# Sliding-window attention and a mixture of adapters on one core: rows of q and k laid on the partitions run by run instead of head by head

## The chip, the cores and the metric

The kernel runs on one core of a Trainium2 chip. The metric is the device time of one execution in microseconds (us); the times of several runs are summed up by their median. The core has TensorE (PE, matrix products; PEld is its weight load), VectorE (DVE), ScalarE (ACT), GpSimd (POOL) and SyncE (SP). SP, ACT and POOL issue the transfers (DMAs), which 16 DMA engines of the core carry out.

## The reference

`q`, `k` and `v` have the shape 8 batches x 8 heads x 576 positions x 64, in float32. The first part is attention in a window of 32 positions to each side, the second a mixture of eight low-rank adapters of which each row takes the best two:

```python
scores = scale * np.matmul(q, k.transpose(0, 1, 3, 2))
mask = np.abs(pos[:, None] - pos[None, :]) <= window          # window = 32
attn = softmax(np.where(mask, scores, -1e9))
x = (attn @ v).transpose(0, 2, 1, 3).reshape(4608, 512)
logits = x @ w_gate                                            # 8 experts
# the two largest logits of a row, softmax over the two: w
out = x + sum over the two experts e of  w_e * (x @ A[e]) @ B[e]    # A: 512x16, B: 16x512
```

## The kernel before, in words

**Tiling.** The batches are taken in two groups (`g` = 0, 1; four batches each), and a step handles one batch `s` of each group, for all eight heads: four steps, `s` = 0 to 3. The 576 positions of a batch are cut into tiles: for each `s` a tile t = 2s (256 positions) and t = 2s + 1 (the next 256), and one more tile, t = XT = 8, that holds the 64 left-over positions of all batches and heads together.

**Loads of q and k** (`run_parts`, `load_qk`; DMA issue in line 308). The rows of a tile are cut in runs of eight positions, 8 x 64 x 4 B = 2 KB in one piece. Even and odd runs go to two buffers (`f` = 0, 1), and for each of them and each group there is one DMA: 128 runs on 128 partitions, 256 KB. For t < 8 the 128 runs are 8 heads by 16 runs, and line 286 puts the head outermost: partition = 16 h + n. For t = XT there are 32 (batch, head) pairs by 4 runs (k, 256 KB) or by 2 runs (q, which takes 32 positions from each end, 64 partitions, 128 KB). In all there are 64 DMAs of 256 KB for t < 8, and 4 of 256 KB and 8 of 128 KB for XT. All are issued by SP, one after the other, in a queue that also holds the 40 stores of the output (line 648).

**From the load to the scores.** A cast to float16 (`cast`: line 321 on POOL or DVE, line 319 on ACT) puts both groups beside each other in `c16`; TensorE transposes it in eight products of 128 x 128 against the identity matrix `ident` (line 329), so that the 64 features stand on the partitions and the partition number of the load becomes the column; ACT or DVE copies the result from PSUM to `qT` or `kT` (line 345). Then, for each step and each of nine key blocks, TensorE writes the mask (line 416) and the scores of all heads (line 422) to PSUM, ACT takes the exponential (line 428), TensorE multiplies with v (line 468), DVE normalises (lines 480, 487).

**Loads of v** (`load_v`, line 373): four DMAs of 128 KB (as written) for each tile, issued by POOL, converted to float16 on the way, then turned by DVE (line 381).

**Adapters** (`moe`): TensorE turns the normalised rows (513), multiplies them with gate and A (553), DVE and ACT work out the gates (563 to 594), TensorE turns again (603), multiplies with B (627) and, from s = 1 on, adds x by a product with the identity (630); ACT or DVE copies to `ob` (638, 641), SP stores.

**What sets the order.** Every operation is entered in a plan with an index. Three tables written out by hand or by a search, `ORDER`, `ON` and `HOME`, say in which order the operations are issued, which of two engines takes one that either can do, and which buffer each tile lives in (9 buffers `raw`, 6 `c16`, 3 `v16`, 8 PSUM banks). Each engine works through its own instructions strictly in that order.

Of the kernel before, what the change touches and what calls it, by code (L numbers as in the profile page):

```python
# [9 lines left out]
F16 = mybir.dt.float16  # L10
F32 = mybir.dt.float32
AF = mybir.ActivationFunctionType
ALU = mybir.AluOpType
# [5 lines left out]
NH = 8  # L19
# [35 lines left out]
class Plan:  # L55
# [14 lines left out]
    def op(self, eng, dur, fn, bufs=(), need=(), make=(), prio=0.0, dma=0.0, mode=0, count=0, desc=0):  # L70
        eng = eng if isinstance(eng, dict) else {eng: dur}
        o = Op(eng, fn, list(bufs), list(need), list(make), prio, dma)
        o.mode, o.count, o.desc = mode, count, desc
        self.ops.append(o)
        for b in o.bufs:
            b.ops.append(o)
        for m in o.make:
            self.makers.setdefault(m, []).append(o)
        return o
# [24 lines left out]
def kernel(  # L104
# [50 lines left out]

    ident = sb.tile([128, 128], F16, name="ident")
    twice = sb.tile([128, 128], F16, name="twice")
    mask0 = sb.tile([128, 128], F16, name="mask0")
    mask = sb.tile([128, 128], F16, name="mask")
    wgf = sb.tile([128, 4, E], F32, name="wgf")  # L160
# [12 lines left out]
    def mm(n): return n / 2400.0 + 0.0035  # L173
# [8 lines left out]


    op("POOL", 0.6, lambda: make_identity(nc, ident), make=["ident"], prio=-99)

    def build_mask():
        nc.gpsimd.memset(mask0, 0.0)
# [91 lines left out]
    def run_parts(w, t, f):  # L279

        r = []
        for g in range(2):
            x = grows[w][g]
            if t < XT:
                r0 = 256 * (t % 2) + (32 if w == "q" else 0)
                i = x[t // 2, :, r0:r0 + 256].rearrange("h (n f r) d -> f h n (r d)", f=2, r=8)[f]
                r.append((g, 0, 128, i))
            elif w == "k":
                i = x.rearrange("b h n d -> (b h) n d")[:, 512:576].rearrange(
                    "u (n f r) d -> f u n (r d)", f=2, r=8)[f]  # L290
                r.append((g, 0, 128, i))
            else:
                for e in range(2):
                    i = x.rearrange("b h n d -> (b h) n d")[:, 544 * e:544 * e + 32].rearrange(
                        "u (n f r) d -> f u n (r d)", f=2, r=8)[f]
                    r.append((g, 64 * e, 64, i))
        return r

    def load_qk(w, t):
# [5 lines left out]
        for hf in range(2):  # L305
# [21 lines left out]
            def trans(c16=c16, tp=tp):  # L327
                for r in range(8):
                    nc.tensor.matmul(out=ap16(tp)[:, 128 * r:128 * r + 128], lhsT=ap(c16)[:, r],  # L329
                                     rhs=ident, is_transpose=True, start=True, stop=True)  # L330
            pr = due - 22 + late + 0.1 * hf
            op("PE", 8 * mm(128), trans, bufs=[c16, tp], need=[(w, t, hf, "16"), "ident"],
               make=[(w, t, hf, "T")], prio=pr, count=8)

            def evict(eng, hf=hf, tp=tp):
# [333 lines left out]
def BY_PE(s, w, j):  # L669
# [2 lines left out]


ORDER = (
# [31 lines left out]
)  # L706
ON = (
    "000011100000010000110010000000000000000001000000000000010100100000001000001000001000010000"
    "001000110010000000000000000000000000000100010100100000010000000100000000000010001010000100"
    "000000000000000000000000000000000000000000000000000100000000000000010000000000000000010000"  # L710
    "000000000000010010010000000010000000000000010000000000000000101100000000101000010000000000"
    "000000010000000000000000000000000000000000100000011010000000000000100000100100000000000000"
    "000000100100000000000000000000000001000001000000000000000000000000000000010000000000000000"
    "000000000000000000000000000000000000010000010000000000"
)
HOME = (
# [13 lines left out]
)  # L730


# [28 lines left out]
```

## Time and profile before

| | |
|---|---|
| median of three runs | 178.53 us (176.23 to 179.34) |
| profiled execution, its own time | 178.09 us |
| its span | 176.3 us, so 1.8 us lie around the span |
| PE busy | 123.9 us (70%) |
| DVE, ACT, POOL busy | 89.9, 86.3, 50.9 us |
| mean granted clock of PE | 0.868 |
| bytes from and to memory | 28.85 MB read, 9.44 MB written |

The span is counted from the first instruction. "DMA" in a list of slices or windows is the mean busy share of the 16 DMA engines (1.00: all of them, all the time), GB/s what they moved. In a row of the timeline the two numbers ahead are the start and the length in us; a row of several instructions says how many ("x3"). The chain is the work that ended last, followed back to what released it.

### The profile page before, as it was taken

How to read it: one execution, taken by the hardware profiler on the slowest of the kernel's cores; microseconds unless marked ns; L12 is line 12 of the kernel's file. 1: busy time of each engine (PE TensorE's matmuls, PEld its weight loads, DVE VectorE, ACT ScalarE, POOL GpSimd, SP SyncE). 2: the span in 40 equal slices, each digit the busy share in tenths (PEclk: the TensorE clock that was granted, in tenths of full speed). 3: DMA queues.
4: the chain of work that ended last, by engine and by line, in shares of the span. 5: the costliest groups of instructions: out<-in, count | busy, mean ns of one | idle time of the engine just before them, and what ended most of it. 6: DMA issues, size and time to landing. Idle time of an engine off the chain costs nothing.

```text
span 176.3 us, 5204 instructions
## 1 busy us (share of the span) xinstructions
PE 123.9 (70%) x2206; PEld 89.6 (51%) x2206; DVE 89.9 (51%) x186; ACT 86.3 (49%) x123; POOL 50.9 (29%) x85
## 2 busy tenths in 40 slices
PE   4800487629619879469998997807947999986660
PEld 2200465526419757456588765504736776675220
DVE  3002182703612797184998675521235959767720
ACT  4000356334802768155866876307345779742540
POOL 8700006284237368002403580029602000000000
PEclk9995559975985999957999999965699999999997
DMA  3876656779659569865556669778939030373086
GB/s 108 192 185 221 180 184 221 216 211 232 152 187 241 159 204 227 190 242 211 204 208 256 229 191 244 264 277 272 231 101 321 0 122 14 124 231 106 26 308 204
DMA packets 19272, 33.91 MB, mean 192 GB/s; under 512 B 4145, under 2 KB 4145, under 8 KB 19249
## 3 DMA queue, kind: packets, MB, share of 16 engines
q1 hardware_dynamic: 15168, 28.32, 45.7%
q0 software_dynamic: 2752, 4.72, 15.8%
q10 hardware_dynamic: 1328, 0.54, 1.1%
q8 instruction: 17, 0.28, 0.6%
q14 instruction: 7, 0.05, 0.1%
HBM read 28.85 MB, written 9.44 MB: 217 GB/s over the span
## 4 chain that ended last, share of the span: by engine, by line
DMA 58%; PE 24%; DVE 7%; SPq 3%; ACT 3%; issue 1%; POOLq 1%; DVEq 0%; ACTq 0%
DMA raw<-in_q_dram 35%; DMA raw<-in_k_dram 23%; PE banks L422 5%; PE banks L468 4%; SPq L308 3%; PE banks L513 3%; PE banks L627 3%; PE banks L329 3%; PE banks L416 3%; DVE xb L487 2%; PE banks L630 2%; PE banks L553 1%; DVE ob L641 1%; PE banks L603 1%; DVE zs L594 1%
## 5 line engine op out<-in xcount | busy, mean ns | idle before, releaser
L321 POOL CAST c<-raw 128x1024 f16<-128x1024 f32 x26 | 27.1, 1053 | 82.1 <-DMA raw<-in_q_dram 37.3
L329 PE MATMUL banks<-ident,c 128*128 128x128 f16 x288 | 26.2, 251 | 26.5 <-ACT c L319 15.1
L428 ACT ACTIVATE PT<-banks 128x1024 f16<-128x1024 f32 x36 | 35.7, 1025 | 10.0 <-PE banks L422 9.6
L329 PEld LDWEIGHTS <-c 128*128 128x128 f16 x288 | 21.0, 113 | 30.2 <-ACT c L319 16.6
L422 PE MATMUL banks<-qT,kT 64*64 64x128 f16 (+1 forms) x576 | 24.5, 230 | 1.2 <-ACT qT L355 1.0
L422 PEld LDWEIGHTS <-kT 64*64 64x64 f16 x576 | 18.7, 116 | 10.9 <-issue 9.9
L381 DVE STREAM_TRANSPOSE vt<-v 128x1024 f32<-128x1024 f32 x9 | 18.6, 2063 | 10.9 <-DMA v<-in_v_dram 10.9
L638 ACT COPY ob<-banks 128x1024 f32<-128x1024 f32 x13 | 13.0, 1013 | 18.5 <-issue 7.4
L416 PE MATMUL banks<-mask,twice 64*128 64x512 f16 x72 | 15.6, 427 | 8.5 <-ACT ob L638 7.3
L319 ACT CAST c<-raw 128x1024 f16<-128x1024 f32 x7 | 7.3, 1045 | 27.3 <-DMA raw<-in_k_dram 14.3
L468 PE MATMUL banks<-vt,PT 64*128 64x65 f16 x832 | 17.8, 194 | 3.8 <-ACT ob L638 2.4
L373 POOL DMA_DIRECT2D v<-in_v_dram x36 | 19.6, 559 | 0.0
L468 PEld LDWEIGHTS <-PT 64*128 64x128 f16 x832 | 15.0, 96 | 7.7 <-issue 6.0
L487 DVE TENSOR_TENSOR xb<-banks,rc 128x768 f16<-128x768 f32 x16 | 15.1, 956 | 2.0 <-PE banks L513 1.5
L627 PE MATMUL banks<-Bw,zT 128*128 128x512 f16 x40 | 15.0, 396 | 1.4 <-DVE zT L179 0.7
L480 DVE RECIPROCAL rc<-banks 128x12 f32<-128x12 f32 (+1 forms) x28 | 6.2, 220 | 15.5 <-PE banks L468 15.3
L487 DVE TENSOR_TENSOR xa<-banks,rc 128x640 f16<-128x640 f32 (+1 forms) x12 | 10.4, 869 | 5.8 <-PE banks L513 5.3
L345 ACT COPY qT<-banks 128x512 f32<-128x512 f32 x13 | 7.6, 590 | 11.8 <-PE banks L329 11.8
L181 ACT COPY xT<-banks 128x512 f32<-128x512 f32 x16 | 9.2, 588 | 6.7 <-PE banks L513 6.6
L553 PE MATMUL banks<-WA,xT 128*128 128x136 f16 x160 | 11.7, 232 | 0.2 <-ACT xT L181 0.2
L321 DVE CAST c<-raw 128x1024 f16<-128x1024 f32 x3 | 2.1, 694 | 18.6 <-DMA raw<-in_q_dram 18.6
L553 PEld LDWEIGHTS <-xT 128*128 128x128 f16 x160 | 10.5, 103 | 1.4 <-issue 0.6
(58 smaller groups left out, 126.2 us busy)
## 6 DMA issues: line engine op xcount, KB each, us to landing
raw<-in_k_dram SPq DMA_DIRECT2D x36, 256.0 KB
raw<-in_q_dram SPq DMA_DIRECT2D x32, 256.0 KB
out_dram<-ob SPq DMA_DIRECT2D x24, 256.0 KB
v<-in_v_dram POOLq DMA_DIRECT2D x36, 128.0 KB, 6.7
out_dram<-ob SPq DMA_DIRECT2D x16, 192.0 KB
raw<-in_q_dram SPq DMA_DIRECT2D x8, 128.0 KB
ob<-in_moe_B_dram ACTq DMA_DIRECT2D x1, 256.0 KB
ob<-in_moe_A_dram ACTq DMA_DIRECT2D x1, 256.0 KB
```

Source lines behind the costliest of these rows:

```text
L321: (nc.vector if eng == "DVE" else nc.gpsimd).tensor_copy(out=o, in_=i)
L329: nc.tensor.matmul(out=ap16(tp)[:, 128 * r:128 * r + 128], lhsT=ap(c16)[:, r], rhs=ident, is_transpose=True, start=True, stop=True)
L373: op("POOL", 0.5, lambda p0=p0, src=src: nc.gpsimd.dma_start(out=ap(v16)[p0:p0 + 32], in_=src), bufs=[v16], make=[("v", t, "16")], prio=-6 ...
L381: nc.vector.transpose(out=o, in_=i)
L416: nc.tensor.matmul(out=p[:, 4 * j:4 * j + 4], lhsT=twice[m], rhs=bcast(mask[m], 1, 4), start=True, stop=False)
L422: nc.tensor.matmul(out=p[m, h, c0:c0 + hi - lo], lhsT=ap(kT[t])[m, 64 * sl:64 * sl + 64], rhs=ap(qT[s])[m, h, lo:hi], start=False, stop=h ...
L428: op("ACT", act(1024), lambda: nc.scalar.activation(out=ap(pt)[:, :, 64:192].rearrange("m i (x b r) -> m i x b r", b=2, r=16), in_=ap(ps). ...
L468: nc.tensor.matmul(out=ap(po)[:, 512 * g + VD * j:512 * g + VD * j + VD], lhsT=ap(PT[ti])[m, pos, off:off + 128], rhs=ap(vt[t])[m, sl, 0:V ...
L487: nc.vector.tensor_tensor(out=o, in0=i, in1=ap(rc)[:, 0:n].to_broadcast([128, n, 2, D]), op=ALU.mult)
L553: nc.tensor.matmul(out=ap(pz)[:, o:o + ER + E], lhsT=ap(xT)[:, i, c, :], rhs=WA[:, c, :], start=(c == 0), stop=(c == 3))
L627: nc.tensor.matmul(out=o, lhsT=ap(zT)[:, j + i], rhs=Bw, start=True, stop=not by_pe)
L638: (nc.vector.tensor_copy if eng == "DVE" else nc.scalar.copy)(out=ap(ob)[:, 0:m], in_=i0)
```

## The change: 16 runs by 8 heads

For t < 8, the source of a load is now read as (run, head) instead of (head, run): run n of head h goes to partition 8 n + h. The DMAs keep their number, their 256 KB and their 2 KB pieces. So that the columns after the transpose are in the old order, the transposes of these tiles take a permutation matrix `swap` instead of `ident`; it is built once on POOL by a memset and one selection. XT keeps its layout and `ident`.

The three tables are new as a whole. On POOL, the constants are now built ahead of all loads of v, in the order mask, `ident`, `swap`, `twice`. On SP, the eight loads of t = 0 and the eight of q for XT are now the first 16 loads; before, one load of k for XT stood ahead of the last of them. Casts stay 26 on POOL, 7 on ACT and 3 on DVE; the copies to `ob` go from 13 on ACT and 2 on DVE to 11 and 4; ahead of the last load on SP stand 13 stores instead of 12. On PE, the last transpose for q or k is followed by 504 products instead of 458. Nothing else is changed; lines behind 157 move down by one and those behind 185 by some ten.

```diff
+    swap = sb.tile([128, 128], F16, name="swap")
...
+    def build_swap():
+
+        nc.gpsimd.memset(swap, 0.0)
+        blk = swap.rearrange("p (h n) -> p h n", n=16)
+        nc.gpsimd.affine_select(out=blk, in_=blk, compare_op=ALU.not_equal, fill=1.0, base=0,
+                                channel_multiplier=1, pattern=[[-1, NH], [-NH, 16]])
+    op("POOL", 0.6, build_swap, make=["swap"], prio=-98.5)
...
             if t < XT:
                 r0 = 256 * (t % 2) + (32 if w == "q" else 0)
-                i = x[t // 2, :, r0:r0 + 256].rearrange("h (n f r) d -> f h n (r d)", f=2, r=8)[f]
+                i = x[t // 2, :, r0:r0 + 256].rearrange("h (n f r) d -> f n h (r d)", f=2, r=8)[f]
...
                     nc.tensor.matmul(out=ap16(tp)[:, 128 * r:128 * r + 128], lhsT=ap(c16)[:, r],
-                                     rhs=ident, is_transpose=True, start=True, stop=True)
+                                     rhs=swap if t < XT else ident, is_transpose=True,
+                                     start=True, stop=True)
...
-            op("PE", 8 * mm(128), trans, bufs=[c16, tp], need=[(w, t, hf, "16"), "ident"],
+            op("PE", 8 * mm(128), trans, bufs=[c16, tp], need=[(w, t, hf, "16"), "ident", "swap"],
...
 ORDER = (
-    26, 23, 3, 24, 12, 10, 9, 34, 15, 40, 35, 0, 63, 6, 61, 45, 4, 39, 18, 36, 30, 29, 19, 62, 44,
...
+    25, 4, 7, 8, 18, 19, 27, 2, 26, 36, 41, 35, 15, 58, 30, 57, 40, 5, 56, 55, 45, 20, 31, 62, 65,
...
```

More of the change, by code (lines that the diff above doesn't have):

```diff
@@ L674 @@
 ORDER = (
[31 rows of a table removed]
[31 rows of a table added]
 )
 ON = (
[L708 to L714, printed above, removed]
+    "001110000000100000000100010001000000010000000010000001000100000000000000000101000100000100"
+    "001000010000000110010000000000000000100000000000000000001000100010000000000000000010000000"
+    "000000000100000000000001000000000000000000000000010001000000000000000101000000000000000000"
+    "001000001000000000000010000000000000000000000100000000000000000000010000100000100000010010"
+    "000100100000001000000000011000001000000000000010000100000000000100000100000100010010000000"
+    "000000000000000000010000000000000000000000100000000000000000000000000000000000000100000000"
+    "0000000000000000000000000000000000000000100000000001000"
 )
 HOME = (
[13 rows of a table removed]
[13 rows of a table added]
 )
```

86 rows, old and new, of tables (HOME, ORDER) are left out of this document.

## The prediction

> **What bounds the kernel now.** I read the page from the top: the busy shares, then the slices, the DMA queues, and the chain that ended last.
>
> ```profile
> span 176.3 us, 5204 instructions
> PE 123.9 (70%) x2206; PEld 89.6 (51%) x2206; DVE 89.9 (51%) x186; ACT 86.3 (49%) x123; POOL 50.9 (29%) x85
> ...
> q1 hardware_dynamic: 15168, 28.32, 45.7%
> q0 software_dynamic: 2752, 4.72, 15.8%
> q10 hardware_dynamic: 1328, 0.54, 1.1%
> ...
> DMA 58%; PE 24%; DVE 7%; SPq 3%; ACT 3%; issue 1%; POOLq 1%; DVEq 0%; ACTq 0%
> DMA raw<-in_q_dram 35%; DMA raw<-in_k_dram 23%; PE banks L422 5%; PE banks L468 4%; SPq L308 3%; PE banks L513 3%; PE banks L627 3%; PE banks L329 3%; PE banks L416 3%; DVE xb L487 2%; PE banks L630 2%; PE banks L553 1%; DVE ob L641 1%; PE
> ```
>
> No compute engine is full, and 58% of the chain is loads of q and k. Yet the DMA engines look idle a third of the time: the three queues sum to 62.6% of 16 engines. The two fit together only if the loads cannot use all engines. So I looked for a stretch in which nothing but these loads is in flight, and found 80 to 94 us. SP issues there:
>
> ```profile
> 79.06 3.23 SPq L308 DMA_DIRECT2D raw<-in_q_dram  x3
> 82.91 1.99 SPq L308 DMA_DIRECT2D raw<-in_k_dram  x2
> 85.62 0.60 SPq L308 DMA_DIRECT2D raw<-in_q_dram  x1
> 86.26 0.60 SPq L308 DMA_DIRECT2D raw<-in_k_dram  x1
> 86.95 2.86 SPq L308 DMA_DIRECT2D raw<-in_q_dram  x3
> 90.36 1.93 SPq L308 DMA_DIRECT2D raw<-in_k_dram  x2
> ```
>
> All are 256 KB loads for t < 8. POOL issues no v between 71 and 99 us. The windows show what that yields, and what stores alone yield (134 to 136 us):
>
> ```profile
> core 0: us, PE busy (x) PEld busy (x) DVE busy (x) ACT busy (x) POOL busy (x), PEclk, DMA share, GB/s
> 14.00:18.00 4.00, 0.00 (x0) 0.00 (x0) 0.17 (x2) 0.66 (x1) 0.00 (x0) 0.50 0.73 222
> 18.00:20.00 2.00, 1.56 (x15) 1.56 (x16) 0.00 (x0) 0.69 (x2) 0.00 (x0) 0.50 0.72 174
> 26.00:28.00 2.00, 2.00 (x37) 1.38 (x36) 0.87 (x1) 1.00 (x2) 1.31 (x2) 0.69 0.52 200
> 80.00:94.00 14.00, 13.46 (x315) 10.06 (x313) 11.24 (x19) 9.03 (x11) 3.08 (x3) 0.93 0.54 205
> 134.00:136.00 2.00, 1.88 (x70) 1.73 (x71) 0.56 (x2) 1.07 (x2) 0.06 (x1) 1.00 1.02 385
> ```
>
> For 14 us the share sits at 0.54 and the rate at 205 GB/s, as at 26 us (0.52, 200): half the engines, all the time. Stores reach 1.02 and 385 GB/s. The share goes well over a half only with stores, with v, or with the 128 KB loads of XT (14 to 20 us). The loads with a share of a half are those whose source has 8 heads outermost; the stores and XT have 96 or 128 rows, or 32 (batch, head) pairs, outermost. So half the DMA engines bound the kernel up to the last load, with which this stretch of the chain ends:
>
> ```profile
> 120.35 12.52 DMA raw<-in_k_dram
> ...
> 134.12 0.62 PE banks L329 x8
> ```
>
> After it come 43 us in which loads play no part. The three long stretches:
>
> ```profile
> 25.00:133.00 108.00, 81.18 (x1537) 61.42 (x1534) 57.73 (x113) 57.82 (x85) 42.92 (x59) 0.85 0.71 215
> 75.00:110.00 35.00, 31.41 (x646) 23.92 (x647) 26.57 (x58) 23.71 (x34) 10.69 (x14) 0.90 0.66 223
> 133.00:157.00 24.00, 23.03 (x545) 16.60 (x543) 18.17 (x33) 16.91 (x23) 1.04 (x1) 1.00 0.33 118
> ```
>
> From 133 to 157 us PE is full: 545 products in 24 us, 22.7 a us. While loads bind (25 to 133 us) it does 1537 in 108 us, 14.2 a us.
>
> **The change part by part.**
>
> *Loads.* With 16 runs outermost I expect each load for t < 8 to spread over all 16 engines. At 205 GB/s the 64 loads of 262,144 B take 81.8 us; at the stores' 385 GB/s, 43.6 us. So 38 us leave the path at most, and only as far as something else does not fill the room. [...]
>
> *Stage A, to the first score (25.40 us before).*
>
> ```profile
> 25.40 0.61 PE L416 MATMUL banks<-mask,twice 64*128 64x512 f16 x2
> ```
>
> ```profile
> L319 ACT CAST c<-raw 128x1024 f16<-128x1024 f32 x7 | 7.3, 1045 | 27.3 <-DMA raw<-in_k_dram 14.3 <-DMA raw<-in_q_dram 13.0
> L345 ACT COPY qT<-banks 128x512 f32<-128x512 f32 x13 | 7.6, 590 | 11.8 <-PE banks L329 11.8
> ```
>
> ```profile
> 0.00:10.00 10.00, 5.93 (x8) 2.28 (x8) 1.62 (x8) 1.99 (x3) 6.91 (x25) 1.00 0.67 158
> 22.00:25.00 3.00, 2.26 (x22) 1.89 (x21) 2.18 (x5) 1.41 (x2) 0.00 (x0) 0.50 0.60 183
> ```
>
> The start of the first score, the two groups of hand-over work (busy, mean ns) and two windows: the engines move some 4.4 MB in the first 25 us (158 GB/s at first, 174 to 222 later). XT's loads, wide already, the weights and v are among them, so I take the middle of 205 and 385, 295 GB/s: 15 us, plus 2 us until the flow stands, plus cast 1.05, transposes 0.62, copy 0.59: 19.3, called **20 us**. Ends: 16 (all at 385) and 25.4.
>
> *Stage B, to the last load (25 to 133 us before).* The DMA engines' own work there is 0.71 x 108 = 77 us at full width; PE's 1537 products at 22.7 a us need 68 us. Neither runs without gaps. From 75 to 110 us, where loads bound less, PE did 646 in 35 us, 18.5 a us; at that pace 1537 take **83 us**. It is the nearest row to a mixture of loads, casts and scores, so I take it. Ends: 77 (DMA full) and 108.
>
> *Stage C, from the last load to the end.* 176.3 - 133 = 43.3 us. The new order leaves 504 products behind the last transpose instead of 458; 46 at 22.7 a us are 2 us: **45 us**. Ends 43 and 47. It contains a serial tail (157 to 176 us) that nothing here shortens.
>
> *The transposes.* 256 of the 288 take `swap` in place of `ident`: same shape, same type, same count. Two dense stretches bound the difference:
>
> ```profile
> 96.02 0.92 PE banks L513 x16
> 96.94 0.45 PE banks L329 x8
> ```
>
> 57.5 and 56 ns each for transposes of other data: 256 x 1.5 ns is 0.4 us either way. I take 0.
>
> *POOL at the start.* `swap` adds a memset and a selection:
>
> ```profile
> masks.py:199 POOL TENSOR_SCALAR_AFFINE_SELECT ident<-ident 128x128 f16<-128x128 f16 x1 | 0.3, 289 | 0.1
> masks.py:197 POOL MEMSET ident<- 128x128 f16 x1 | 0.2, 206 | 0.3 <-POOLq L745 0.3
> ```
>
> ```profile
> 3.73 0.71 POOL L373 DMA_DIRECT2D v<-in_v_dram  x1
> 13.12 0.69 DVE L321 CAST c<-raw 128x1024 f16<-128x1024 f32 x1 [10.67 <-DMA raw<-in_q_dram]
> 24.90 1.97 DVE L381 STREAM_TRANSPOSE vt<-v 128x1024 f32<-128x1024 f32 x1
> ```
>
> 0.5 us, done by about 4 us, while the first cast starts at 13.12 us (some 9 after): hidden. The first load of v, at 3.73 us, falls behind all constants, by 2.5 us; its four pieces end behind two of another tile. The DVE turn that needs it ran at 24.90 us: hidden now. If stage A shrinks to 16, up to 2 us may show. SP keeps its 76 loads and 40 stores in one queue; 13 stores instead of 12 stand ahead of the last load, and a store that waits for its copy holds the loads behind it. One more is worth 0.5 us at the 0.3 to 0.5 us that one takes to issue, or a wait for the copy, up to 2 us; it lies inside stage B's ends. Two copies to `ob` moving from ACT to DVE (1.0 against 1.2 us each) meet engines busy half the time: 0.
>
> *Sum.* 20 + 83 + 45 = 148 us of span against 176.3; with the 1.8 us around it, **150 us** against the profiled execution's 178.09. The median, 178.53, is 0.4 us above that; I leave this out. Of the 38 us that the loads could give, 28 come through, because PE is next: in stage B its floor (68) and the DMA floor (77) are close.
>
> **The rivals.**
>
> *Wide reads run slower per engine.* In the windows from 14 to 20 us, with XT loads in the mixture, a share of 0.73 gave 222 and one of 0.72 gave 174 GB/s: weighted, 206 at 0.73, or 282 GB/s at full share, against 205 / 0.54 = 380 for the narrow loads alone. At 282 the 64 loads take 59.5 us, a gain of 22 instead of 38; in proportion 28 x 22/38 = 16 us of span: **162 us**. For it: those two rows. Against: stores at 385, and XT reads its heads outermost, which the new loads do not. The same 157 to 170 would come if PE, casts and copies hand over worse than from 75 to 110 us (16 products a us give 96 us for stage B, 163 in all).
>
> *Slower.* If the 16 engines, reading pieces 4 KB apart at the same time, hinder each other so that a wide load moves less than 205 GB/s, the change loses: that is the turning point. At the 174 of the 18 to 20 us row the 64 loads take 96.4 us, 14.6 more than now; in the same proportion +11 us: **189 us**. Nothing but that one short row, at a share of 0.72, speaks for it, and its rate per engine (174 / 0.72 = 242 at full share) is still above the turning point.
>
> *The loads do not widen.* If the spread over engines does not come from the outermost dimension, the share stays near 0.54 and only the order differs: **174 to 182 us**. Against: two kinds of load on the same queue, from the same tensors, that differ in that dimension and in the share.
>
> *Better.* If stage B reaches the DMA floor of 77 and stage A 16 us: 16 + 77 + 45 + 1.8 = **140 us**.
>
> **How the numbers follow.** Forecast, 142 to 157 us: 0.55. Wide reads slower or a worse hand-over, 157 to 172: 0.28. Below 142: 0.06. No widening, 174 to 182: 0.06. Slower: 0.05. The predicted time is 150 us. The range reaches from 140 to 170: it leaves out some 0.05 below, 0.03 of the second case, and the last two. About 2% (3.6 us) is what a measurement of this kernel can tell from no change, the three runs lying 1.7% apart. Faster by more than that: 0.89; within: 0.06; slower: 0.05.
>
> **What would show it.** Right: a window with loads for t < 8 alone has a DMA share near 1 and over 330 GB/s; the first score starts near 20 us; the last load lands near 103 us; PE does 18 products a us between them; DMA's part of the chain falls well below 58% and PE's rises. Wrong: a share near 1 with under 300 GB/s (slow wide reads), a share that stays near 0.54 (no widening), or loads that are through early with PE still at 14 to 16 products a us, which would put the bound in the order or in the casts and copies.

## The result, and the profile after

The changed kernel takes 148.27 us (median of 4 runs, 147.79 to 149.54), the kernel before beside it 178.03 (176.23 to 179.34): a ratio of 0.837 with a 95% interval of 0.827 to 0.846. The ratio is taken over executions with an undisturbed clock, so that it can differ a little from the quotient of two medians. The forecast was 150 us. The profiled execution took 149.54 us, with a span of 147.8.

The page of the changed kernel: busy shares, the two DMA rows of the 40 slices, the queues and the chain that ended last.

```profile
span 147.8 us, 5212 instructions
PE 117.6 (80%) x2206; PEld 85.0 (58%) x2206; DVE 90.4 (61%) x185; ACT 84.9 (57%) x123; POOL 51.6 (35%) x88
...
DMA  4999999999999999999999999999911030940484
GB/s 128 256 225 254 266 254 297 283 258 254 271 273 273 275 240 277 268 286 347 326 278 322 302 301 290 145 266 293 332 40 49 27 113 0 320 150 0 170 311 160
...
q1 hardware_dynamic: 15680, 28.32, 63.5%
...
PE 54%; DMA 20%; DVE 13%; ACT 3%; issue 3%; POOL 2%; SPq 0%; DVEq 0%; ACTq 0%; POOLq 0%
```

PE now has the largest part of the chain, and loads have 20% of it instead of 58% (14 points of the 20 are loads of q and k, 6 are loads of v). The DMA engines are full from 4 to 107 us (90% or more in every slice). But look at q1, the queue of all q and k loads and of all stores. It moves the same 28.32 MB as before and takes more engine time for them: 63.5% of 147.8 us is 93.9 us, against 45.7% of 176.3, which is 80.6 us. The loads have become wide (a share of 1.07 in the first two windows below, 0.54 before), and each engine has become slower: it takes longer for the same bytes.

Windows of the changed kernel (start and end, length, busy time and count of each engine, granted clock, DMA share, GB/s). In the first row only loads of q and k for t < 8 move; in the second also three loads of k for XT, which SP issues between them. Then come stages B and C of the prediction, and the same time cut at 25, 65 and 105 us:

```profile
core 0: us, PE busy (x) PEld busy (x) DVE busy (x) ACT busy (x) POOL busy (x), PEclk, DMA share, GB/s
20.00:25.00 5.00, 4.24 (x43) 3.04 (x41) 3.80 (x6) 2.22 (x3) 1.04 (x1) 0.52 1.07 293
22.00:30.00 8.00, 7.14 (x120) 4.98 (x120) 2.95 (x5) 5.64 (x7) 4.77 (x7) 0.82 1.07 292
23.80:104.50 80.70, 71.72 (x1474) 54.89 (x1474) 55.78 (x110) 54.76 (x80) 41.56 (x58) 0.95 1.04 279
104.50:147.80 43.30, 33.39 (x688) 22.78 (x680) 28.18 (x60) 23.22 (x33) 1.04 (x1) 0.96 0.39 134
...
0.00:25.00 25.00, 13.72 (x74) 8.07 (x74) 7.62 (x17) 7.49 (x11) 9.73 (x30) 0.73 0.98 239
25.00:65.00 40.00, 32.12 (x689) 25.90 (x684) 24.58 (x48) 25.78 (x39) 21.51 (x32) 0.92 1.06 265
65.00:105.00 40.00, 38.91 (x796) 28.60 (x793) 30.46 (x65) 28.39 (x41) 19.82 (x27) 0.99 1.02 293
```

The same cut of the kernel before:

```profile
25.00:65.00 40.00, 27.71 (x523) 21.21 (x520) 18.48 (x33) 19.61 (x30) 18.85 (x26) 0.80 0.71 201
65.00:105.00 40.00, 35.25 (x691) 27.21 (x690) 29.03 (x59) 25.38 (x37) 15.06 (x22) 0.91 0.68 217
```

The timeline of the changed kernel has the edges of the stages: the cast whose transposes stand ahead of the first score on PE, the first DVE turn of v, the first score, and the last cast of q, which starts when the last load has landed.

```profile
21.62 1.04 ACT L328 CAST c<-raw 128x1024 f16<-128x1024 f32 x1 [0.93 <-DMA raw<-in_q_dram]
...
23.45 1.99 DVE L391 STREAM_TRANSPOSE vt<-v 128x1024 f32<-128x1024 f32 x1
...
23.69 0.61 PE L426 MATMUL banks<-mask,twice 64*128 64x512 f16 x2
...
104.53 1.04 POOL L330 CAST c<-raw 128x1024 f16<-128x1024 f32 x1 [6.96 <-DMA raw<-in_q_dram]
```

Stage A went from 25.4 to 23.7 us, stage B (first score to last load) from 107.6 to 80.8, stage C stayed at 43.3. So 26.8 of the 28.5 us of span were gained between the first score and the last load.

### The profile page after: what moved, and what is told of

Same layout as the page of the kernel before. It is cut to its first block, busy times and chain, and to the rows that moved or that the text cites. A ratio compares the mean times of both kernels' runs of the same rounds, so it can differ in the third digit from the quotient of the medians.

```text
span 147.8 us, 5212 instructions
## 1 busy us (share of the span) xinstructions
PE 117.6 (80%) x2206; PEld 85.0 (58%) x2206; DVE 90.4 (61%) x185; ACT 84.9 (57%) x123; POOL 51.6 (35%) x88
## 3 DMA queue, kind: packets, MB, share of 16 engines
q1 hardware_dynamic: 15680, 28.32, 63.5%
## 4 chain that ended last, share of the span: by engine, by line
PE 54%; DMA 20%; DVE 13%; ACT 3%; issue 3%; POOL 2%; SPq 0%; DVEq 0%; ACTq 0%; POOLq 0%
PE banks L432 11%; DMA raw<-in_q_dram 9%; PE banks L338 8%; PE banks L478 8%; PE banks L426 6%; DMA v<-in_v_dram 6%; PE banks L523 6%; PE banks L637 5%; PE banks L563 5%; DMA raw<-in_k_dram 4%; DVE xb L497 4%; PE banks L640 3%; DVE vt L391 3%; PE banks L613 2%; DVE ob L648 1%
## 5 line engine op out<-in xcount | busy, mean ns | idle before, releaser
L338 PEld LDWEIGHTS <-c 128*128 128x128 f16 x288 | 20.2, 111 | 12.6 <-ACT c L328 8.5
L338 PE MATMUL banks<-swap,c 128*128 128x128 f16 x256 | 21.2, 242 | 6.9 <-ACT c L328 4.7
L432 PE MATMUL banks<-qT,kT 64*64 64x128 f16 (+1 forms) x576 | 22.2, 218 | 0.6 <-ACT qT L355 0.4
L432 PEld LDWEIGHTS <-kT 64*64 64x64 f16 x576 | 16.8, 108 | 10.2 <-issue 9.3
L637 PE MATMUL banks<-Bw,zT 128*128 128x512 f16 x40 | 14.4, 381 | 1.7 <-ACT zT L182 1.7
L426 PE MATMUL banks<-mask,twice 64*128 64x512 f16 x72 | 14.9, 390 | 0.5 <-ACT qT L355 0.4
L648 ACT COPY ob<-banks 128x1024 f32<-128x1024 f32 x11 | 11.1, 1020 | 4.0 <-PE banks L640 3.4
L355 ACT COPY kT<-banks 128x512 f32<-128x512 f32 x13 | 7.7, 589 | 6.5 <-PE banks L338 6.5
L563 PE MATMUL banks<-WA,xT 128*128 128x136 f16 x160 | 10.8, 223 | 0.0
L497 DVE TENSOR_TENSOR xa<-banks,rc 128x640 f16<-128x640 f32 (+1 forms) x12 | 10.3, 862 | 0.3
L563 PEld LDWEIGHTS <-xT 128*128 128x128 f16 x160 | 9.6, 98 | 0.6
```

What stands on the lines that cost most here:

```text
L355: (nc.vector.tensor_copy if eng == "DVE" else nc.scalar.copy)(out=o, in_=i)
L426: nc.tensor.matmul(out=p[:, 4 * j:4 * j + 4], lhsT=twice[m], rhs=bcast(mask[m], 1, 4), start=True, stop=False)
L432: nc.tensor.matmul(out=p[m, h, c0:c0 + hi - lo], lhsT=ap(kT[t])[m, 64 * sl:64 * sl + 64], rhs=ap(qT[s])[m, h, lo:hi], start=False, stop=h ...
L497: nc.vector.tensor_tensor(out=o, in0=i, in1=ap(rc)[:, 0:n].to_broadcast([128, n, 2, D]), op=ALU.mult)
L563: nc.tensor.matmul(out=ap(pz)[:, o:o + ER + E], lhsT=ap(xT)[:, i, c, :], rhs=WA[:, c, :], start=(c == 0), stop=(c == 3))
L637: nc.tensor.matmul(out=o, lhsT=ap(zT)[:, j + i], rhs=Bw, start=True, stop=not by_pe)
```

## The experiments

**Is it the layout or the new order?** The change does two things: it turns the source of the loads round, with the permutation that this needs, and it brings new tables of order, engines and buffers. One kernel takes the layout back and keeps the tables; the other puts the layout, and the building of `swap`, into the kernel before.

```
# changed kernel, old layout
-  x[...].rearrange("h (n f r) d -> f n h (r d)", f=2, r=8)[f]
+  x[...].rearrange("h (n f r) d -> f h n (r d)", f=2, r=8)[f]
-  rhs=swap if t < XT else ident
+  rhs=ident
# kernel before, new layout: the same two lines the other way round,
# and swap built in the operation that builds ident
```

> The changed kernel with its new tables, but with the old layout: heads outermost in the source and the identity in every transpose. Theory (the layout spreads a load over 16 DMA engines instead of 8, and that is the whole gain): with q and k loads alone in flight the DMA share falls back to 0.52 to 0.55 and the rate to about 205 GB/s, the last load lands near 130 us, time 172 to 186 us, no better than the kernel before. Rival (the new tables made the gain): 148 to 155 us.

> The kernel before with its old tables, but with the new layout and the permutation (built in the same operation as the identity). Theory (the layout makes the gain, the order follows the data): share near 1.0 with q and k loads alone, 280 to 300 GB/s, time 148 to 158 us. Rival (the old order, made for slow loads, holds the loads back behind casts and stores): 160 to 172 us. Rival (the tables made the gain): 175 us or more.

Old layout with new tables: 173.5 us (172.63 to 174.36) against 177.81, ratio 0.982 (0.973 to 0.991). New layout with old tables: 152.61 (151.32 to 153.87), ratio 0.861 (0.850 to 0.872). The windows of the first, with loads for t < 8 alone, and its chain:

```profile
22.00:26.00 4.00, 2.87 (x24) 2.40 (x24) 2.68 (x4) 1.63 (x2) 0.00 (x0) 0.50 0.53 201
68.00:72.00 4.00, 0.42 (x24) 0.29 (x19) 3.95 (x5) 0.00 (x0) 2.15 (x3) 0.89 0.53 204
```

```profile
DMA 68%; PE 9%; DVE 8%; SPq 7%; issue 2%; ACT 1%; POOLq 1%; DVEq 0%; ACTq 0%
```

With the layout taken back the share is 0.53 again, the rate 201 to 204 GB/s, and DMA has 68% of the chain. The layout alone brings 0.139 x 177.8 = 24.7 us. The tables bring about 3 us alone, and the remaining 4 on top of the layout (0.861 to 0.837, two measurements whose intervals, 0.850 to 0.872 and 0.827 to 0.846, do not quite meet). The section on the change calls the load of k that stood ahead of the last of q for XT one of XT; by the plan it is one of t = 1.

**Does the outermost dimension of the source set the number of engines?** A kernel of loads and stores alone, in groups of 256 KB loads that differ in how the source is cut.

```
four           "b (p x) -> b p x"              4 outermost
heads_by_runs  "h (n f r) d -> f h n (r d)"    8  (as before)
runs_by_heads  "h (n f r) d -> f n h (r d)"   16  (as changed)
pairs_by_runs  "b h (n f r) d -> f (b h) n (r d)"  16 pairs outermost
whole          "(p x) -> p x"                128
```

> No computation at all, the output is not the reference's: 256 KB loads of 2 KB pieces, in six stretches with a full wait between them, then 36 stores. The outermost dimension of the source is 4 (batches), 8 (heads), 16 (runs, two batch groups in turn as in the changed kernel), 16 (runs, one batch group), 16 (batch-head pairs, each with 8 runs), 128 (256 KB in one piece). Theory (the outermost count sets the number of engines): 4 gives a share of 0.25 and about 102 GB/s, 8 gives 0.52 and 205, 16 and 128 a share of 1.0. Rival (heads lying 147 KB apart are slow, whatever the count): 4 is not slower than 8, and 16 batch-head pairs stay near 205. For the rate of the wide loads, 290 GB/s in the changed kernel: if the interleaving of the two batch groups costs it, one batch group gives over 350; if neighbouring engines reading pieces 4 KB apart cost it, pairs and the whole piece give over 350; if reads simply stop near 290, all of them stay at 280 to 300.

Its windows, one for each number of outermost rows, the stores last. The columns are those of the engines that do anything, then clock, DMA share and GB/s:

```profile
core 0: us, DVE busy (x) POOL busy (x), PEclk, DMA share, GB/s
4.00:12.00 8.00, 0.92 (x6) 0.00 (x0) 1.00 0.26 102
22.00:34.00 12.00, 2.66 (x18) 0.00 (x0) 1.00 0.52 200
66.00:88.00 22.00, 6.79 (x45) 0.00 (x0) 1.00 1.07 266
94.00:100.00 6.00, 2.77 (x18) 0.00 (x0) 1.00 1.01 355
106.00:122.00 16.00, 0.00 (x0) 0.00 (x0) 1.00 1.05 405
```

4 outermost give a DMA share of 0.26, 8 one of 0.52, 16 one of 1.07 and 128 one of 1.01: by the share a quarter, a half and all of the engines. (The row of 16 holds two kinds, runs by heads and pairs by runs.) The pages of the two kernels fit this in a second way: q1 has 15680 packets instead of 15168 for the same bytes, 512 more, which is eight for each of the 64 loads, as many as the step from half of 16 engines to all of them adds. That the outermost dimension sets the share is shown, and with it the mechanism of the change. What the share does not tell is the last column: from 8 to 16 the rate rises from 200 to 266 only, so that a full share is worth 249 GB/s (266 / 1.07) instead of 385 (200 / 0.52). From here on the question was why.

**What do the loads still cost?** The changed kernel, with only the first half of each 2 KB piece of q and k loaded. The packets are as many as before and half as long (15680 in q1 again, for 18.88 MB instead of 28.32, stores included).

```
-  out=ap(raw)[p0:p0 + np_, g], in_=src
+  out=ap(raw)[p0:p0 + np_, g, 0:256], in_=src[:, :, 0:256]
   # the other half of each raw buffer is set to zero once
```

> The changed kernel with only the first half of each 2 KB piece of q and k loaded (the rest of the buffers is set to zero once at the start on VectorE, some 4 us of memsets), so that the q and k loads move half the bytes in as many transfers; all compute stays. Theory A (after the change the DMA engines, full from 10 to 100 us, still set the pace to the last load): the last load lands 12 to 20 us earlier and the time falls to 128 to 137 us. Theory B, the prediction's term (TensorE and the hand-over of casts and copies set the pace at 18 products a us): the time stays at 143 to 148 us.

139.28 us (2 runs), ratio 0.788 (0.778 to 0.798): about 9 us less than the changed kernel, between what the two theories had expected. Its windows:

```profile
0.00:25.00 25.00, 15.37 (x144) 8.98 (x144) 12.31 (x26) 10.99 (x15) 12.41 (x34) 0.93 0.72 178
25.00:65.00 40.00, 35.34 (x830) 26.89 (x830) 33.47 (x58) 29.25 (x45) 24.00 (x34) 1.00 0.86 205
65.00:105.00 40.00, 38.70 (x824) 29.27 (x822) 29.04 (x65) 28.88 (x42) 15.28 (x22) 1.00 0.70 182
```

By 65 us it has done 144 + 830 = 974 products, the changed kernel 74 + 689 = 763. The 211 more are worth 10.6 us at the 19.9 a us (796 in 40) that the changed kernel does after 65 us; the spans differ by 10.2. After 65 us the two hardly differ (824 and 796). So loads still hold PE back, but only in the first 65 us; then PE is busy for 38.9 or 38.7 of 40 us whether the DMA share is 1.02 or 0.70. The number of products is a rough measure, as they differ in length, and part of the gain is clock: from 25 to 65 us PE is busy for 3.2 us more and is granted 1.00 instead of 0.92; over the whole span a transpose with `swap` takes 219 ns instead of 242.

Through which wait the loads hold PE back can be read from the chain of the changed kernel. Its last DMA is this one, a load of v, with DVE's turn and the products that wait for it behind:

```profile
29.67 8.80 DMA v<-in_v_dram
38.50 2.05 DVE vt L391
40.59 0.70 PE banks L478 x34
```

It belongs to tile t = 1. POOL issues it at 29.15 us, behind casts of k and q in its order, and it takes 8.8 us to land while the loads of q and k keep the engines full. With half the bytes the same load is issued 3.9 us earlier and takes 5.97 us, and PE waits for the turn 1.3 instead of 2.6 us:

```profile
33.80 0.70 PE L478 MATMUL banks<-vt,PT 64*128 64x65 f16 x34 [1.30 <-DVE vt L391]
```

In these traces, then, the full engines reach PE through a load that waits in POOL's order and lands late. An earlier place for this load of v was not tried.

**Is it the neighbourhood of the pieces in memory?** More loads alone, and the changed kernel with adjacent runs: the 16 runs of one load follow each other in memory (32 KB from each head) instead of every second one, with the permutation to match.

```
runs_by_heads           "h (n f r) d -> f n h (r d)"    every second 2 KB of a head
adjacent_runs_by_heads  "h (f n r) d -> f n h (r d)"    32 KB in one piece of a head
whole                   "(p x) -> p x"                  256 KB in one piece
whole_in_turn           "(a e x) -> e a x", e=16        the same 256 KB, cut 16 by 8
```

> Again loads only, no computation, the output is not the reference's; all loads spread over 16 engines, 4 MB in each of six stretches. Which neighbourhood costs the rate that scattered wide loads lack (265 GB/s against some 350 for whole 256 KB pieces): runs by heads as in the changed kernel (every other 2 KB of a head), the same with adjacent runs (32 KB in one piece per head), 4 KB runs, batch-head pairs with adjacent runs (16 KB in one piece per pair and engine), whole 256 KB, and whole 256 KB dealt out to the engines in turn. Theory A (reading every other 2 KB costs it): adjacent runs and 4 KB runs give over 330, as the whole pieces do. Theory B (jumping between heads 147 KB apart costs it): adjacent runs stay at 260 to 290, pairs too, only the whole pieces give over 330. Theory C (each engine must read in one piece): pairs with adjacent runs and whole pieces are fast, whole in turn is not.

> The changed kernel with the halves of a tile cut differently: buffer 0 holds the first 128 positions of a tile and buffer 1 the second 128, so that a load reads 32 KB in one piece of each head instead of every other 2 KB of 64 KB; the permutation and the copy out of PSUM put the columns where they were. Nothing else changes. If adjacent reads are faster (theory A): loads alone at 330 GB/s or more, the last load some 8 us earlier, time 140 to 145 us. If they are not (theory B): 146 to 150 us.

> The changed kernel itself, on the chip of the run before it, for comparison: 147 to 150 us.

Windows of the loads alone, in the order of the list:

```profile
4.00:13.00 9.00, 3.07 (x27) 0.00 (x0) 1.00 1.01 269
16.00:28.00 12.00, 4.32 (x36) 0.00 (x0) 1.00 1.07 280
...
66.00:73.00 7.00, 3.20 (x27) 0.00 (x0) 1.00 1.05 386
76.00:87.00 11.00, 3.49 (x25) 0.00 (x0) 1.00 1.07 272
```

Adjacent runs move 280 GB/s against 269, and in the kernel they gain nothing: 150.6 us (149.4 to 151.57) against 148.39 (146.02 to 149.17) for the changed kernel on the same chip, ratios 0.857 (0.839 to 0.875) and 0.836 (0.807 to 0.865). Runs of 4 KB (266 GB/s) and pairs with adjacent runs (284), two more groups of the same kernel, do no better. The figures are those of theory B, but the last two rows take its reason away, as neither of them jumps between heads: the very same 256 KB move at 386 GB/s as 128 rows and at 272 as 16 by 8.

**Is it the addresses that are read at one time, or the split?** A third set of loads alone: the same pieces with steps between them, cut as 128, as 32 by 4 and as 16 by 8.

```
every other 2 KB   [(1024, 128)]            128
every other 8 KB   [(4096, 32), (512, 4)]    32 by 4
every other 16 KB  [(8192, 16), (512, 8)]    16 by 8
whole              [(512, 128)]             128
whole in turn      [(512, 16), (8192, 8)]    16 by 8
whole again        [(512, 128)]             128
```

> Loads only again, no computation, the output is not the reference's. It is open why whole 256 KB pieces came at 385 GB/s and every other wide pattern at 265 to 285, the same 256 KB dealt to the engines in turn among them. Six patterns: every other 2 KB (one dimension over the 128 partitions), every other 8 KB (32 by 4), every other 16 KB (16 by 8), whole, whole in turn, whole again from another part. Theory A (what counts is that the source is one dimension over all partitions): every other 2 KB comes at 340 or more like whole, the others at 265 to 285. Theory B (what counts is the piece that one engine reads without a jump): every other 16 KB is as fast as whole, every other 2 KB is not. Theory C (only one unbroken piece is fast): whole and whole again alone are over 340. Whole again at under 300 would say that the place in memory counts.

```profile
8.00:13.00 5.00, 2.45 (x22) 0.00 (x0) 1.00 1.04 392
14.00:23.00 9.00, 4.28 (x37) 0.00 (x0) 1.00 1.06 388
25.00:36.00 11.00, 4.54 (x39) 0.00 (x0) 1.00 1.06 312
40.00:47.00 7.00, 3.54 (x30) 0.00 (x0) 1.00 1.05 387
50.00:61.00 11.00, 4.20 (x37) 0.00 (x0) 1.00 1.06 323
66.00:70.00 4.00, 2.03 (x14) 0.00 (x0) 1.00 1.04 373
```

All three theories for this run fall. Steps cost nothing (392 and 388 with every other piece left out). The two cuts of 16 by 8 are the slow ones, at 312 and 323, and all others have 373 to 392, at the same share. It is the split, then: 16 outermost rows fill all engines (a share of 1.06), but each engine moves less than with 32 or 128. The size of the loss varies: whole in turn, 16 by 8 with the same steps, had moved 272 GB/s in the run before and moved 323 in this one. Why stays open.

**Does the last load set the end?** The prediction added a stage C to the landing of the last load. Here the 13 stores that stand ahead of that load go behind it, with 8 output buffers instead of 4 so that this is possible; the control has the 8 buffers alone.

```
   # after ORDER and ON are read
+  early = [stores ahead of the last load]
+  order = [... without early, up to the last load] + early + [the rest]
-  "ob": 4
+  "ob": 8
```

> The changed kernel with the 13 stores that stand ahead of the last load moved behind it in SP's queue, and 8 instead of 4 buffers for the output so that they can wait. Theory A (the DMA engines, full to 98 us, set the time of the last load; 13 stores are 3.2 MB, 8 us at 390 GB/s): the last cast starts at 94 to 98 us instead of 104, time 140 to 144 us. Theory B (casts, copies and TensorE set it by now): 146 to 149 us.

> The changed kernel with 8 output buffers and the stores where they were, the control of the run before: 146 to 149 us by both theories.

148.85 us (148.14 to 150.0), ratio 0.839 (0.832 to 0.847); the control 149.85 (148.87 to 150.99), ratio 0.845 (0.838 to 0.851). Last cast of the kernel with the stores behind, and of the control:

```profile
94.12 1.06 POOL L343 CAST c<-raw 128x1024 f16<-128x1024 f32 x1
```

```profile
104.39 1.04 POOL L343 CAST c<-raw 128x1024 f16<-128x1024 f32 x1 [5.42 <-DMA raw<-in_q_dram]
```

The last cast starts 10.3 us earlier, and the time stays within the scatter of the control. So the landing of the last load does not set the end in the changed kernel. In both chains the last DMA is again a load of v, which lands at 57.4 us and, in the control, at 59.2. In the kernel before, the chain ran through that landing; whether it set the end there was not tried.

**A version with 32 outermost.** If the split into 16 by 8 is what slows the engines, and the loads bind up to 65 us, then 32 runs of 4 heads should be faster. Buffer f then holds heads 4f to 4f + 3 with all 32 runs, instead of every second run of all heads; the permutation and the copies behind the transposes follow.

```
-  x[...].rearrange("h (n f r) d -> f n h (r d)", f=2, r=8)[f]
+  x[t // 2, 4 * f:4 * f + 4, r0:r0 + 256].rearrange("h (n r) d -> n h (r d)", r=8)
-  pattern=[[-1, NH], [-NH, 16]]                 # swap
+  pattern=[[-1, 4], [-16, 8], [-8, 2]], base=-4 * f, for f = 0, 1
```

> The changed kernel with 32 adjacent runs outermost and 4 heads within a load, instead of 16 by 8: buffer 0 of a tile holds heads 0 to 3, buffer 1 heads 4 to 7; the permutation and the copies put the columns where they were. Loads alone moved 385 GB/s with 128 or 32 by 4 pieces, 265 to 325 with 16 by 8. Theory A (a split 32 by 4 runs at full rate in the kernel too, and the DMA engines hold TensorE back only up to about 65 us): 360 GB/s or more with q and k loads alone, the first score at 20 to 22 us, time 142 to 145 us. Theory B (the rate of the loads no longer matters to the end, as for the last load): 147 to 150 us. Theory C (the rate hangs on jumps between heads, not on the split): still below 300 GB/s and 147 to 150 us.

> The changed kernel itself beside the run before it, on the same chip, so that the two can be compared: 147 to 150 us by all theories.

144.91 us (6 runs, 143.79 to 145.82), ratio 0.815 (0.809 to 0.821). The changed kernel beside it: 149.77 (6 runs, 146.22 to 151.19), ratio 0.829 (0.817 to 0.840). The medians lie 4.9 us apart; the ratios differ by 0.0137, which is 2.4 us of 178.7, and their intervals overlap by 0.003. All six times lie below all six of the changed kernel, so it comes out as the fastest of the three, by some 2.4 us if one goes by the ratios; the overlap leaves the size uncertain. Its queue q1, and its windows (in the first only loads of q and k move, some of them of XT, and the source of each has 32 outermost):

```profile
q1 hardware_dynamic: 15680, 28.32, 58.2%
```

```profile
20.00:26.00 6.00, 5.33 (x77) 3.51 (x76) 3.13 (x5) 3.85 (x5) 2.39 (x4) 0.73 1.06 387
...
0.00:25.00 25.00, 13.87 (x96) 8.21 (x96) 8.05 (x17) 8.93 (x13) 10.64 (x32) 0.80 0.96 273
25.00:65.00 40.00, 33.91 (x742) 26.90 (x743) 26.93 (x52) 27.12 (x42) 22.84 (x32) 0.91 0.95 277
```

387 GB/s where 16 by 8 had 292 or 293, and q1 needs 58.2% of 143.4 = 83.5 us of engine time, near the 80.6 of the kernel before. By 65 us this kernel has done 838 products, 75 more than the changed one: 3.8 us at 19.9 a us, of the 4.4 by which the spans differ. (These are two single traces of times that scatter by some us.) From 25 to 65 us its DMA share is 0.95 and PE is still busy for only 33.9 of 40 us. More than half of the 6.1 us is one wait, again for the turn of v for t = 1:

```profile
38.25 1.12 PE L482 MATMUL banks<-vt,PT 64*128 64x65 f16 x34 [3.50 <-DVE vt L395]
```

## Why the prediction was right

The sum came out almost to the digit, 147.8 us of span against 148, but not term by term: 23.7 + 80.8 + 43.3 against 20 + 83 + 45. That the misses of +3.7, -2.2 and -1.7 us cancel is luck.

*Loads, the mechanism: right.* 16 outermost rows use all engines (1.07 against 0.54), shown by the loads alone and by taking the layout back.

*Loads, the size: wrong.* This is the term that was mis-sized. The prediction took the stores' 385 GB/s for reads on all engines: 43.6 us for the 64 loads. They moved 292, so 16.78 MB need 57.5 us; in two later traces of the same kernel they moved 260 and 263 from 20 to 25 us, where this one has 293, and at 260 they would need 64.5 us. By the prediction's own list, a share near 1 with under 300 GB/s was the sign of its first rival, slow wide reads, and its rate of 282 was the better one, though by luck: it came from narrow loads mixed with those of XT, and reads are not slow for being wide. The reason that the prediction leaned on, that reads can do what stores do, holds for other splits: 373 to 392 GB/s with 32 or 128 outermost in the third set of loads alone, against the 385 that it took from the stores.

*Why the rival's time of 162 us was wrong although its rate was right.* It reduced the whole gain of 28 us in proportion to the loads' gain (22/38). But 28 was already what PE let through, not what the loads gave. With the loads at 292 GB/s there were still 24 us to give. (This is an account by sums and not a measurement; at 260 GB/s it gives 17 us, and those traces are no longer than 148.6 us.) After 65 us PE is full and takes nothing more from faster loads, as half the bytes show (824 products against 796). So the loss of 14 us in the loads cost no 12 us, but what 32 outermost gets back, some 2.4 us by the ratios and 4.9 by the medians.

*Stage A: 23.7 instead of 20.* Same term. By the time of the cast ahead of the first score (21.6 us) some 4.9 MB had moved: 10 us at 199 GB/s, 6 at 254 and 5.6 at 256, with all engines busy from 10 us on:

```profile
0.00:10.00 10.00, 6.45 (x8) 2.52 (x8) 2.52 (x9) 2.39 (x4) 8.69 (x29) 1.00 0.86 199
10.00:16.00 6.00, 1.03 (x8) 0.77 (x8) 0.00 (x0) 1.67 (x2) 0.00 (x0) 0.60 1.07 254
16.00:22.00 6.00, 3.57 (x31) 3.04 (x32) 2.59 (x4) 2.17 (x5) 0.00 (x0) 0.50 1.07 256
```

The prediction had 4.4 MB at 295. Its range of 16 to 25.4 holds the result.

*Stage B: 80.8 instead of 83.* The pace of 18.5 products a us, taken from the row in which loads bound least, came out at 18.3 (1474 in 80.7); the rest is the count, 1474 instead of 1537. That is a good pace found for a partly wrong reason. The prediction set it between a DMA floor of 77 us and a PE floor of 68. The DMA floor was really 1.04 x 80.7 = 83.9 us of engine time, so the engines were full all through. By the run with half the bytes, DMA held PE back up to 65 us and not after; the last DMA on the chain is the load of v that lands at 38.5 us, a wait that the prediction had in no step.

*Stage C: 43.3 instead of 45.* The 2 us for 46 more products did not show. The step itself, last load plus C, was right as arithmetic and wrong as a cause: with the last load 10.3 us earlier the time is the same. It held because PE, too, was full at that point: busy for 38.9 of the 40 us up to 105.

*The transposes, cost 0: right.* Group of transposes before (all 288 with `ident`) and after (the 256 with `swap`), the mean in ns behind the comma:

```profile
L329 PE MATMUL banks<-ident,c 128*128 128x128 f16 x288 | 26.2, 251 | 26.5 <-ACT c L319 15.1
```

```profile
L338 PE MATMUL banks<-swap,c 128*128 128x128 f16 x256 | 21.2, 242 | 6.9 <-ACT c L328 4.7
```

242 against 251 ns, at a mean granted clock of 0.919 instead of 0.868, and the idle time ahead of them fell from 26.5 to 6.9 us.

*POOL at the start and the stores: hidden, as costed.* The first load of v is issued at 6.19 us, 2.5 later as costed; its DVE turn starts at 23.45 us, ahead of the first score, and the first product with v at 29.82, so the building of `swap` delayed nothing that shows. Moving all 13 stores out of the loads' way gained nothing measurable. That the tables themselves bring 3 to 4 us was in no step of the prediction.

*The rivals.* No widening and slower are excluded by the share and by the undoing of the line. The turning point of the slower one, wide loads under 205 GB/s, was never near: the lowest rate of 16 by 8 alone was 266. The better one (140) had stage B at a DMA floor of 77 us; the floor was 83.9.

## What to carry to other kernels

When a long stretch of loads sits at a fraction of the DMA share, look at how many rows the source has outermost: 8 had a share of 0.52 here, 16 one of 1.06 at 312 and 323 GB/s, and 32 or 128 one of 1.04 to 1.06 at 373 to 392. So a share near 1 does not tell the bandwidth: read GB/s beside it, in a window with one kind of transfer. And after a bound is lifted, ask where it still binds: here faster loads paid before 65 us and not after, and the last DMA on the chain was a load of v, whose layout the change had left alone.

## What the runs showed that was not expected

- At a DMA share of 1.01 to 1.07, loads split 16 by 8 moved 266 to 323 GB/s, and loads of the same size split 32 by 4 or 128 moved 355 to 392, with the same bytes in one case (386 against 272). Steps between the pieces made no difference. The cause is open: no run here shows it.
- A last cast that starts 10.3 us earlier (94.1 against 104.4 us) changed nothing that the scatter lets one see.
- Between 25 and 65 us PE was busy for 32.1 us instead of 27.7, and the granted clock there was 0.92 instead of 0.80, so some of PE's faster pace can be clock.
